# More accumulator banks for the feed-forward steps around a tile's end, and attention steps of the first two blocks laid out anew

## The chip, the cores and the metric

The kernel runs on one core of one Trainium2 chip. The metric is the device time of that core in microseconds (us), the median of three runs. Five engines work side by side: TensorE (PE; its weight loads are shown apart as PEld), VectorE (DVE), ScalarE (ACT), GpSimd (POOL) and SyncE (SP). Transfers run on DMA engines that all issuers share. TensorE writes its results to PSUM, eight banks of 128 x 512 float32; VectorE and ScalarE read them there.

## The reference

Attention over a window of the last 96 keys and the first 8 ("global") keys, with a linear distance bias, and then a gated feed-forward layer on the result:

```python
# q, k, v: (batch 4, heads 8, seq 768, dim 64)
scores = scale * q @ k.T  + bias            # bias = -slope[h] * distance
scores = where(keep, scores, -1e9)          # keep: local (0 <= i-j < 96) or global (j < 8)
a = exp(scores - max); a = a / (sum(a) + 1e-9)
attn = a @ v
x = attn as (3072 tokens, 512)
g = x @ w_gate                              # 512 x 1536
out = (g * sigmoid(g)) * (x @ w_val) @ w_out   # 1536 x 512
```

## The kernel before

The 3072 tokens are 8 tiles of 384 (two per batch element, here "block"). A tile takes 12 feed-forward steps, one for each 128 of the 1536 features. A step is four matmuls for the gate (`gps`), four for the value (`vps`), and then ScalarE and VectorE:

```python
def products(t, f, which, c0, c1, dst=None):
    ...
        if dst is None:
            dst = spare("gv"[which] + "ps")        # a bank, from the rotation "x"
    w = (wg, wv)[which]
    for c in range(c0, c1):
        nc.tensor.matmul(gv[f, which][:, 0:TB], lhsT=w[:, c, 128*f:128*f+128],
                         rhs=x_of(t)[:, c, :], start=(c == 0), stop=(c == NC - 1))

def gate_or_val(t, f, which, c0=0):
    products(t, f, which, c0, NC)
    dst = gv.pop((f, which))
    if which == 0:
        th = ...; nc.scalar.activation(out=th, in_=dst[:, 0:TB], func=AF.Tanh, scale=0.5)
        sl = ...; nc.vector.scalar_tensor_tensor(out=sl, in0=th, scalar=1.0,
                      in1=dst[:, 0:TB], op0=AluOp.add, op1=AluOp.mult)   # reads the gate's bank
    else:
        nc.vector.tensor_mul(hTs[t][:, f, :], dst[:, 0:TB], gv["sl"])    # reads the value's bank
```

`th` and `sl` have two buffers each. The banks: three (`x0` to `x2`) rotate for gates and values, four (`a0` to `a3`) for attention, and `o0` takes the output matmuls (`ops`):

```python
state = {"tags": ["a0", "a1", "a2", "a3"], "n": 0, "x": ["x0", "x1", "x2"]}

def spare(name, dt=FP32):
    tag = state["x"][gv.get("n", 0) % len(state["x"])]
    gv["n"] = gv.get("n", 0) + 1
    return single(name, tag, dt)          # waits until the tag's last readers are done
```

A list `later` holds VectorE, ScalarE and GpSimd work that is taken up piece by piece between steps. The attention of a block half ends with `values`: denominators (`den`) and numerators (`num`), copied to `ns` by ScalarE; VectorE turns the denominators (`dT`), inverts (`dR`), spreads them (`rb`) and scales, which gives the x of the next tile:

```python
later.append(lambda: self.invert(den))    # dT, dR
later.append(spread)                      # rb
if mul_eng is not nc.gpsimd:
    for side in range(2):
        later.append(lambda side=side: scale_num(side))   # xT
```

Block 0 is worked in two halves. Its second half is turned (transposed on TensorE, then copied from PSUM to `kT` and `qT`) pair by pair, two pairs sharing two banks; k and q of one pair lie in different banks:

```python
def trh(*units):
    def step():
        ks, qs = single("trs", "o0", FP16), spare("trs", FP16)
        for i, (hp, k_eng, q_eng) in enumerate(units):
            c = slice(TB * i, TB * i + TB)
            pairs[0, hp].transposes_half(1, [qs[:, c], ks[:, c]], k_eng, q_eng)  # turn, then copy
    return step

half1 = {(0, 1): [trh((0, A, A), (1, V, A))], (0, 2): [sch(0)],      # A: ScalarE, V: VectorE
         (0, 3): [sch(1), trh((2, V, A), (3, V, V))], (0, 5): [sch(2)], (0, 6): [sch(3)],
         (0, 7): [va(0, 0, 1)], (0, 8): [va(0, 1, 1)]}
```

A key `(t, f)` names the step of tile t after which the work is put: `sch` and `sc` make scores (with their exponentials and mask products), `va` the values, `tr` turns two pairs of a later block. Block 1 is worked in tile 1's steps; the last number of `ff` says how many groups of three output matmuls go behind each step:

```python
def first(t, b):
    return {(t, 3): [tr(b, 0), tr(b, 1)],
            (t, 5): [sc(b, (0, 0), (0, 1), (1, 0))],
            (t, 7): [tr(b, 2), tr(b, 3)],
            (t, 8): [sc(b, (1, 1), (2, 0), (2, 1))],
            (t, 9): [sc(b, (3, 0), (3, 1))],
            (t, 10): [va(b, 0, 0)], (t, 11, 1): [va(b, 1, 0)]}
...
(ff(1, 0, 6, (0, 0, 0, 1, 0, 1)) + ff(1, 6, 11, (1,)) + [(1, 11, 5)], first(1, 1)),
```

Weights come in four pieces of features (`load_w(0, 2)`, `(2, 4)`, `(4, 8)`, `(8, 12)`), each as two transfers for `wg` and two for `wv`: the first holds the rows of matmuls 0 and 1 of a burst, the second those of 2 and 3.

Of the kernel before, what the change touches and what calls it, by code (L numbers as in the profile page):

```python
# [37 lines left out]
def kernel(  # L38
# [223 lines left out]
    class Pair:  # L262
# [27 lines left out]
                in_=k3[:, 0, NG:2 * NG].unsqueeze(1).broadcast_to([128, NCH, NG]))  # L290


        def transposes_half(self, half, tr, k_eng, q_eng):
            hp = self.hp
            trq, trk = tr
            for st, dst in ((k16, trk), (q16, trq)):
                for j in range(J2):
                    for hi in range(2):
                        nc.tensor.transpose(  # L299
                            dst[64 * hi:64 * hi + 64, 128 * j:128 * j + 128],  # L300
                            st[:, half, 2 * hp + hi, D * j:D * j + D], ident)
            if half == 0:
                self.qT = sb2.tile([128, S], FP16, name="qT", tag="qT", bufs=NP)
                self.kT = kTs[hp]
            k3 = self.kT.rearrange("r (c m) -> r c m", m=128)
            t3 = trk.rearrange("r (j p) -> r p j", j=J2)
            pc = KC // J2
            cut = (TB - 3 * KC) // J2

            def part(c0, c1, m0, m1, p0):  # L310
                n = (m1 - m0) // J2
                k_eng(out=k3[:, c0:c1, NG + m0:NG + m1].rearrange("r c (p j) -> r c p j", j=J2),
                      in_=t3[:, p0:p0 + (c1 - c0) * n, :].rearrange(
                          "r (c p) j -> r c p j", c=c1 - c0))

            if half == 0:
                part(0, 3, 0, KC, 0)
                part(3, 4, 0, cut * J2, 3 * pc)
                nc.vector.tensor_copy(
                    out=k3[:, :, 0:NG],  # L320
                    in_=k3[:, 0, NG:2 * NG].unsqueeze(1).broadcast_to([128, NCH, NG]))
            else:
                part(3, 4, cut * J2, KC, 0)
                part(4, 6, 0, KC, pc - cut)
                part(6, 7, 0, S - 6 * KC, 3 * pc - cut)
            q_eng(
                out=self.qT[:, TB * half:TB * half + TB].rearrange("r (p j) -> r p j", j=J2),
                in_=trq.rearrange("r (j p) -> r p j", j=J2))
# [33 lines left out]
            else:  # L362
                exps()

        def scores(self, bk, mul_eng, put_off, sc):
            hp = self.hp
            for c in range(NCH):
                cb, col, q0, n = chunks[c]
                if cb != bk:
                    continue  # L370
                for hi in range(2):
                    r = slice(64 * hi, 64 * hi + 64)
                    keys = (kE[r, hp, :] if c == J and self.b > 1
                            else self.kT[r, 128 * c:128 * c + 128])
                    nc.tensor.matmul(  # L375
                        sc[hi][:, col:col + n], lhsT=keys,
                        rhs=self.qT[r, q0:q0 + n], start=True, stop=True)
            at = sb2.tile([128, 2, BANK], FP16, name="at", tag=f"at{bk}", bufs=NP)
            self.at[bk] = at

            def exps():
                for hi in range(2):
                    nc.scalar.activation(out=at[:, hi, :], in_=sc[hi][:, 0:BANK],  # L383
                                         func=AF.Exp, scale=scale)

            def mask():
                m = masks[:, 2 * hp:2 * hp + 2, :]
                if bk == 1:
                    for i in range(2):
                        a2 = at[:, :, WIN * i:WIN * i + WIN]  # L390
                        mul_eng.tensor_mul(a2, a2, m[:, :, WIN:2 * WIN])  # L391
                else:
                    o = WIN // 2 * bk
                    mul_eng.tensor_mul(at, at, m[:, :, o:o + BANK])  # L394

            if put_off:
                later.append(exps)
            else:
                exps()
            later.append(mask)  # L400

        def transposes_dma(self):
            b, hp = self.b, self.hp
# [8 lines left out]
    class Quad:  # L412
# [49 lines left out]
        def values(self, half, bank, mul_eng):  # L462
            den = bank("den")
            self.weigh(half, den, None)
            srcs = []
            for side in range(2):
                num = bank("num")
                self.weigh(half, num, side)
                src = sb2.tile([128, TB], FP32, name="ns", tag="ns", bufs=4)
                nc.scalar.copy(out=src, in_=num[:, 0:TB])  # L470
                srcs.append(src)

            def scale_num(side):
                mul_eng.tensor_mul(self.x_out(half, side), srcs[side], self.rb)  # L474

            def spread():
                self.spread()
                if mul_eng is nc.gpsimd:
                    for side in range(2):
                        scale_num(side)  # L480

            later.append(lambda: self.invert(den))
            later.append(spread)
            if mul_eng is not nc.gpsimd:
                for side in range(2):
                    later.append(lambda side=side: scale_num(side))

        def denominators(self, den):
            self.weigh(0, den, None)
# [8 lines left out]
    def both_values(b, half):  # L498
        two = [quads[b, g] for g in range(2)]
        for quad in two:  # L500
            den = spare("den")
            quad.weigh(half, den, None)
            quad.invert(den)
        srcs = {}
        for g, quad in enumerate(two):
            for side in range(2):
                num = bank("num")
                quad.weigh(half, num, side)
                src = sb2.tile([128, TB], FP32, name="ns", tag="ns", bufs=4)
                nc.scalar.copy(out=src, in_=num[:, 0:TB])  # L510
                srcs[g, side] = src

        def scale_num(eng, g, side):
            eng.tensor_mul(two[g].x_out(half, side), srcs[g, side], two[g].rb)  # L514

        def spread_first():
            two[0].spread()
            for side in range(2):
                scale_num(nc.gpsimd, 0, side)

        later.append(spread_first)
        later.append(two[1].spread)
        for side in range(2):
            later.append(lambda side=side: scale_num(nc.vector, 1, side))

    hTs = {}

# [86 lines left out]

    def p_tr(hp, kt, qt, q_eng):
        tr = [single("trs", t, FP16)[:, 0:TB] for t in (qt, kt)]
        pairs[0, hp].transposes_half(0, tr, V, q_eng)

    V, A = nc.vector.tensor_copy, nc.scalar.copy
    fill(16)  # L620
# [56 lines left out]
    def sc(b, *units):  # L677
        def step():
            for i, (hp, bk, *other) in enumerate(units):
                pair = pairs[b + 1 if other else b, hp]  # L680
                on_vector = pair.b < 2 or bk < 2 or hp % 2 == 0
                pair.scores(bk, nc.vector if on_vector else nc.gpsimd, bool(later),
                            [spare("sc") for _ in range(2)] if len(units) == 3 and i == 0
                            else banks("sc"))
        return step

    def va(b, g, half):
        return lambda: quads[b, g].values(half, bank, nc.vector if b < 2 else nc.gpsimd)

    def vas(b, half):  # L690
        return lambda: both_values(b, half)
# [1 line left out]
    def tr(b, hp):  # L693
        return pairs[b, hp].transposes

    def trh(*units):
        def step():
            ks, qs = single("trs", "o0", FP16), spare("trs", FP16)
            for i, (hp, k_eng, q_eng) in enumerate(units):
                c = slice(TB * i, TB * i + TB)  # L700
                pairs[0, hp].transposes_half(1, [qs[:, c], ks[:, c]], k_eng, q_eng)
        return step

    def sch(hp):
# [13 lines left out]
        return step  # L718

    def first(t, b):  # L720
        return {(t, 3): [tr(b, 0), tr(b, 1)],
                (t, 5): [sc(b, (0, 0), (0, 1), (1, 0))],
                (t, 7): [tr(b, 2), tr(b, 3)],
                (t, 8): [sc(b, (1, 1), (2, 0), (2, 1))],
                (t, 9): [sc(b, (3, 0), (3, 1))],
                (t, 10): [va(b, 0, 0)],
                (t, 11, 1): [va(b, 1, 0)]}
# [11 lines left out]
    def second(t, b):  # L739
        return {(t, 0): [sc(b, (0, 2), (1, 2))], (t, 3): [sc(b, (2, 2), (3, 2))],  # L740
                (t, 7): [vas(b, 1)]}

    half1 = {(0, 1): [trh((0, A, A), (1, V, A))], (0, 2): [sch(0)],
             (0, 3): [sch(1), trh((2, V, A), (3, V, V))], (0, 5): [sch(2)], (0, 6): [sch(3)],
             (0, 7): [va(0, 0, 1)], (0, 8): [va(0, 1, 1)]}

    def ff(t, f0, f1, n_out=(0,)):
# [1 line left out]

    stretches = [  # L750
        (ff(0, 0, 12), half1),
        (ff(1, 0, 6, (0, 0, 0, 1, 0, 1)) + ff(1, 6, 11, (1,)) + [(1, 11, 5)], first(1, 1)),
        (ff(2, 0, 12, (1,)) + ff(3, 0, 12, (1,)), both(2, 1)),
        (ff(4, 0, 12, (1,)) + ff(5, 0, 12, (1,)), both(4, 2)),
        (ff(6, 0, 12, (1,)), second(6, 3)),
# [25 lines left out]
            at_step(int(when) // NFF, int(when) % NFF, it)  # L781

    outs = [(t, i, part) for t in range(NT - 1) for i in range(3) for part in range(4)]
    def take(step_list):
        run_later(len(later))
        for step in step_list:
# [2 lines left out]
    for tiles, steps in stretches:  # L789
        for t, f, n_out in tiles:  # L790
            for ld in loads.pop((t, f), []):
                ld()
            if f == 0:
                run_later(len(later))
            for which in range(2):
                run_later(1)
                gate_or_val(t, f, which, NC if t == 0 and f < 2 else 0)
# [50 lines left out]
```

The softmax here doesn't subtract the row's maximum and nothing guards it: scores larger than these inputs give would overflow.

## Time and profile before

| | |
|---|---|
| time, median of three (least to most) | 245.12 us (245.11 to 245.51) |
| span of the profiled execution | 243.8 us |
| TensorE clock granted | 1.000 |
| idle of VectorE before `sl`, waiting for ScalarE's `th` | 40.1 us in all |
| idle of ScalarE before `th`, waiting for the gate burst | 52.0 us in all |
| DMA from memory | 28.67 MB |

An instruction's line in the timeline gives start, length, engine, source line, operation, what it writes and reads, the shapes, how many alike were merged, and in brackets the idle time of the engine before it with what ended that. A matmul's length is modelled and overlaps the next one's, so the pace of TensorE is read from starts. Line 299 turns block 0's halves, 539 makes gates and values, 552 and 556 are `sl` and `hT`, 375 scores, 213 weight transfers.

### The profile page before, as it was taken

Reading aid. Unit: us, or ns where it says so; the run is one execution under the profiler, and the core shown is the slowest. Engines: PE = TensorE matmul, PEld = TensorE weight load, DVE = VectorE, ACT = ScalarE, POOL = GpSimd, SP = SyncE. Lnnn points to the kernel's source line nnn. Section 1 sums busy time; section 2 is a strip of 40 time slices with the busy share of each in tenths; the row PEclk is TensorE's granted clock in tenths of the full one; section 3 lists DMA queues with packets and bytes.
Section 4 is the critical chain, followed back from the end, with each engine's and each line's share of the span. In section 5 each row is a group of like instructions: output and inputs, shape, how many; then the busy total and the mean of one; then the engine's idle time right before and its main releaser. Section 6 shows DMA issues by size and latency. Waiting matters only on the chain.

```text
span 243.8 us, 6052 instructions
## 1 busy us (share of the span) xinstructions
PE 235.8 (97%) x2428; PEld 136.0 (56%) x2428; DVE 167.1 (69%) x358; ACT 129.4 (53%) x291; POOL 96.8 (40%) x117
## 2 busy tenths in 40 slices
PE   7899898999999999999999999999999999999994
PEld 4555565566465556555565556555655565555543
DVE  5676749888886768776786658776785568555510
ACT  6637576868763655356446465367346534333221
POOL 8999674738980000996062252800032213000000
PEclk9999999999999999999999999999999999999999
DMA  7999999999996684699309778951101101110122
GB/s 142 167 190 198 180 206 198 205 154 126 153 121 117 122 144 100 42 157 148 60 3 140 143 142 94 66 70 44 46 0 46 43 0 46 44 41 5 43 88 86
DMA packets 84612, 25.10 MB, mean 103 GB/s; under 512 B 72816, under 2 KB 81640, under 8 KB 84584
## 3 DMA queue, kind: packets, MB, share of 16 engines
q0 software_dynamic: 65296, 14.05, 65.9%
q1 hardware_dynamic: 18728, 10.30, 16.7%
q8 instruction: 19, 0.31, 0.6%
q10 hardware_dynamic: 560, 0.36, 0.5%
q14 instruction: 9, 0.07, 0.1%
HBM read 28.67 MB, written 6.29 MB: 143 GB/s over the span
## 4 chain that ended last, share of the span: by engine, by line
PE 84%; DVE 7%; ACT 3%; DMA 2%; issue 1%; POOL 0%; DVEq 0%; POOLq 0%
PE gps L539 24%; PE ops L568 23%; PE vps L539 23%; PE sc L375 3%; PE num L439 3%; DMA q<-in_q_dram 2%; PE den L439 2%; DVE sl L552 2%; DVE hT L556 2%; PE sc L335 2%; DVE xT L474 1%; ACT at L357 1%; PE trs L273 1%; ACT th L550 1%; PE trs L299 1%
## 5 line engine op out<-in xcount | busy, mean ns | idle before, releaser
L552 DVE SCALAR_TENSOR_TENSOR sl<-th,gps 128x384 f32<-128x384 f32 x94 | 52.0, 553 | 40.1 <-ACT th L550 39.1
L539 PE MATMUL gps<-xT,wg 128*128 128x384 f16 x376 | 76.9, 327 | 0.4
L539 PE MATMUL vps<-xT,wv 128*128 128x384 f16 x376 | 76.5, 326 | 0.6 <-DVE sl L552 0.5
L550 ACT ACTIVATE th<-gps 128x384 f32<-128x384 f32 x94 | 46.7, 497 | 53.5 <-PE gps L539 52.0
L568 PE MATMUL ops<-wo,hT 128*128 128x512 f16 x276 | 72.8, 379 | 0.0
L556 DVE TENSOR_TENSOR hT<-vps,sl 128x384 f16<-128x384 f32 x94 | 52.0, 554 | 7.9
L539 PEld LDWEIGHTS <-wg 128*128 128x128 f16 x384 | 35.1, 98 | 31.2 <-issue 2.3
L539 PEld LDWEIGHTS <-wv 128*128 128x128 f16 x384 | 37.5, 98 | 26.8 <-issue 2.1
L568 PEld LDWEIGHTS <-hT 128*128 128x128 f16 x276 | 26.9, 98 | 23.9
L383 ACT ACTIVATE at<-sc 128x432 f16<-128x432 f32 x72 | 33.1, 539 | 12.2 <-PE sc L375 12.2
L514 POOL TENSOR_TENSOR xT<-ns,rb 128x384 f16<-128x384 f32 x10 | 9.8, 997 | 67.5 <-DVE rb L455 56.5
L171 POOL DMA_DIRECT2D vS<-in_v_dram x28 | 24.7, 896 | 5.3 <-DMA kst<-in_k_dram 3.8
L574 ACT ACTIVATE osb<-ops 128x512 f32<-128x512 f32 x23 | 13.7, 597 | 21.9 <-PE ops L568 21.9
L394 POOL TENSOR_TENSOR at<-at,masks 128x864 f16<-128x864 f16 x4 | 7.3, 1822 | 23.8 <-ACT at L383 19.1
L394 DVE TENSOR_TENSOR at<-at,masks 128x864 f16<-128x864 f16 x20 | 12.1, 604 | 5.4 <-ACT at L383 5.4
L194 POOL DMA_DIRECT2D kst<-in_k_dram x16 | 13.9, 885 | 2.3 <-PE vps L539 1.7
L357 ACT ACTIVATE at<-sc 128x432 f16<-128x432 f32 (+2 forms) x32 | 11.7, 445 | 5.6 <-PE sc L346 5.4
L194 POOL DMA_DIRECT2D qst<-in_q_dram x16 | 13.7, 877 | 0.2 <-issue 0.2
L510 ACT COPY ns<-num 128x384 f32<-128x384 f32 x20 | 8.1, 492 | 7.9 <-PE num L439 7.9
L439 PE MATMUL num<-at,vS 128*32 128x216 f16 (+6 forms) x560 | 11.1, 226 | 0.0
L391 DVE TENSOR_TENSOR at<-at,masks 128x432 f16<-128x432 f16 x24 | 8.1, 378 | 4.1 <-ACT at L383 4.1
L449 DVE STREAM_TRANSPOSE dT<-den 128x384 f32<-128x384 f32 x16 | 9.3, 581 | 1.4 <-PE den L439 0.9
(74 smaller groups left out, 180.2 us busy)
## 6 DMA issues: line engine op xcount, KB each, us to landing
out_dram<-osb SPq DMA_DIRECT2D x23, 256.0 KB
vS<-in_v_dram POOLq DMA_DIRECT2D x24, 120.0 KB, 5.4
wo<-in_moe_w_out_dram POOLq DMA_DIRECT2D x4, 384.0 KB, 10.4
qst<-in_q_dram POOLq DMA_DIRECT2D x16, 96.0 KB, 4.3
kst<-in_k_dram POOLq DMA_DIRECT2D x16, 90.0 KB, 4.9
wg<-in_moe_w_gate_dram POOLq DMA_DIRECT2D x4, 256.0 KB, 7.7
wv<-in_moe_w_val_dram POOLq DMA_DIRECT2D x4, 256.0 KB, 7.7
kst<-in_k_dram POOLq DMA_DIRECT2D x2, 384.0 KB, 12.0
```

Of the source, the lines that this page charges most:

```text
L171: nc.gpsimd.dma_start(out=vSs[b][NG:NG + n, c, :, :], in_=v[b, :, KC * c:KC * c + n, :].rearrange("h p d -> p h d"))
L194: nc.gpsimd.dma_start(out=st[b][p0:p0 + n, h // 2, :, h % 2, :], in_=src[b, h, 0:n * J].rearrange("(t p) d -> p t d", p=n))
L357: nc.scalar.activation(out=at[:, hi, 0:col + n], in_=sc[hi][:, 0:col + n], func=AF.Exp, scale=scale)
L383: nc.scalar.activation(out=at[:, hi, :], in_=sc[hi][:, 0:BANK], func=AF.Exp, scale=scale)
L394: mul_eng.tensor_mul(at, at, m[:, :, o:o + BANK])
L439: nc.tensor.matmul(dst[r, o:o + n], lhsT=ones[:, 0:32] if side is None else vals[:, 4 * g + j, side::2], rhs=pairs[b, 2 * g + j // 2].at[c ...
L539: nc.tensor.matmul(gv[f, which][:, 0:TB], lhsT=w[:, c, 128 * f:128 * f + 128], rhs=x_of(t)[:, c, :], start=(c == 0), stop=(c == NC - 1))
L550: nc.scalar.activation(out=th, in_=dst[:, 0:TB], func=AF.Tanh, scale=0.5)
L552: nc.vector.scalar_tensor_tensor(out=sl, in0=th, scalar=1.0, in1=dst[:, 0:TB], op0=AluOp.add, op1=AluOp.mult)
L556: nc.vector.tensor_mul(hTs[t][:, f, :], dst[:, 0:TB], gv["sl"])
L568: nc.tensor.matmul(ops, lhsT=hTs[t][:, f, 128 * i:128 * i + 128], rhs=wo[:, f, :], start=(f == 0), stop=(f == NFF - 1))
L574: nc.scalar.mul(out=osb, in_=ops, mul=0.5)
```

## The change

It has four parts, none of which changes what is computed.

1. Between step 9 of tile 0 and step 2 of tile 1 no output matmuls run and attention leaves its four banks alone. There gates and values rotate over seven banks (three and the four of attention) so that TensorE can run ahead of their readers.
2. At the start of that stretch, work for the next x that still waits in `later` is put ahead of the step's own `sl` and `hT`. At the start of a tile, only what its x needs is flushed.
3. In block 0's second half, all transposes of two pairs are issued ahead of their copies, and the banks are shared out so that one bank is read by few engines. For pairs 0 and 1 ScalarE makes every copy; for pairs 2 and 3 VectorE makes `kT` and ScalarE `qT`.
4. Block 1's turns and scores move one step earlier, so that the last two score steps stand two steps apart. The output groups move with them.

```diff
-        def transposes_half(self, half, tr, k_eng, q_eng):
+        def turn_half(self, half, tr):          # transposes only
...
+        def copy_half(self, half, tr, k_eng, q_eng):
...
-    def trh(*units):
+    def trh(h0, h1, by_engine):
         def step():
-            ks, qs = single("trs", "o0", FP16), spare("trs", FP16)
-            for i, (hp, k_eng, q_eng) in enumerate(units):
-                c = slice(TB * i, TB * i + TB)
-                pairs[0, hp].transposes_half(1, [qs[:, c], ks[:, c]], k_eng, q_eng)
+            b0, b1 = single("trs", "o0", FP16), spare("trs", FP16)
+            (a, b), (c, d) = [(t[:, 0:TB], t[:, TB:2 * TB]) for t in (b0, b1)]
+            k_eng = V if by_engine else A
+            pair_of = [(h0, (c, a)), (h1, (d, b))] if by_engine else [(h0, (b, a)), (h1, (d, c))]
+            for hp, tr in pair_of:
+                pairs[0, hp].turn_half(1, tr)
+            for hp, tr in pair_of:
+                pairs[0, hp].copy_half(1, tr, k_eng, A)
         return step
...
-        return {(t, 3): [tr(b, 0), tr(b, 1)],
-                (t, 5): [sc(b, (0, 0), (0, 1), (1, 0))],
-                (t, 7): [tr(b, 2), tr(b, 3)],
-                (t, 8): [sc(b, (1, 1), (2, 0), (2, 1))],
+        return {(t, 2): [tr(b, 0), tr(b, 1)],
+                (t, 4): [sc(b, (0, 0), (0, 1), (1, 0))],
+                (t, 6): [tr(b, 2), tr(b, 3)],
+                (t, 7): [sc(b, (1, 1), (2, 0), (2, 1))],
                 (t, 9): [sc(b, (3, 0), (3, 1))],
...
-    half1 = {(0, 1): [trh((0, A, A), (1, V, A))], (0, 2): [sch(0)],
-             (0, 3): [sch(1), trh((2, V, A), (3, V, V))], (0, 5): [sch(2)], (0, 6): [sch(3)],
+    half1 = {(0, 1): [trh(0, 1, False)], (0, 2): [sch(0)],
+             (0, 3): [sch(1), trh(2, 3, True)], (0, 5): [sch(2)], (0, 6): [sch(3)],
...
-        (ff(1, 0, 6, (0, 0, 0, 1, 0, 1)) + ff(1, 6, 11, (1,)) + [(1, 11, 5)], first(1, 1)),
+        (ff(1, 0, 5, (0, 0, 0, 0, 1)) + ff(1, 5, 11, (1,)) + [(1, 11, 5)], first(1, 1)),
...
+    def widen():
+        while later:
+            run_later(1)
+        x, n = state["x"], gv["n"]
+        state["x"] = ([x[(n + i) % 3] for i in range(3)]
+                      + [state["tags"][(state["n"] + i) % 4] for i in range(4)])
+        gv["n"] = 0
+
+    def narrow():
+        assert gv["n"] % 7 == 3
+        state["x"] = state["x"][0:3]
+        gv["n"] = 0
+
+    at_step(0, 9, widen)
+    at_step(1, 2, narrow)
...
             if f == 0:
-                run_later(len(later))
+                while any(fn.__name__ in ("spread", "spread_first", "scale") for fn in later):
+                    run_later(1)
```

Left out: the renaming that lets pieces of `later` be told apart, and who scales values of later blocks in a path that no later block takes.

More of the change, by code (lines that the diff above doesn't have):

```diff
@@ L301, in transposes_half @@
                             st[:, half, 2 * hp + hi, D * j:D * j + D], ident)
+        def copy_half(self, half, tr, k_eng, q_eng):
+            trq, trk = tr
+            hp = self.hp
             if half == 0:
@@ L363, in scores_half, with scores @@
                 exps()
-        def scores(self, bk, mul_eng, put_off, sc):
+        def scores(self, bk, mul_eng, sc):
             hp = self.hp
@@ L394, in mask @@
                     mul_eng.tensor_mul(at, at, m[:, :, o:o + BANK])
[L396 to L400, printed above, removed]
+            return exps, mask
         def transposes_dma(self):
@@ L473, in scale_num @@
             def scale_num(side):
-                mul_eng.tensor_mul(self.x_out(half, side), srcs[side], self.rb)
+                eng = mul_eng if side else nc.vector
+                eng.tensor_mul(self.x_out(half, side), srcs[side], self.rb)
             def spread():
@@ L478, in spread, with scale @@
                 if mul_eng is nc.gpsimd:
-                    for side in range(2):
-                        scale_num(side)
+                    scale_num(1)
             later.append(lambda: self.invert(den))
             later.append(spread)
-            if mul_eng is not nc.gpsimd:
-                for side in range(2):
-                    later.append(lambda side=side: scale_num(side))
+            for side in range(1 if mul_eng is nc.gpsimd else 2):
+                def scale(side=side):
+                    scale_num(side)
+                later.append(scale)
         def denominators(self, den):
@@ L521, in both_values, with spread, scale @@
         later.append(spread_first)
-        later.append(two[1].spread)
+        def spread():
+            two[1].spread()
+        later.append(spread)
         for side in range(2):
-            later.append(lambda side=side: scale_num(nc.vector, 1, side))
+            def scale(side=side):
+                scale_num(nc.vector, 1, side)
+            later.append(scale)
     hTs = {}
@@ L616, in p_tr @@
         tr = [single("trs", t, FP16)[:, 0:TB] for t in (qt, kt)]
-        pairs[0, hp].transposes_half(0, tr, V, q_eng)
+        pairs[0, hp].turn_half(0, tr)
+        pairs[0, hp].copy_half(0, tr, V, q_eng)
     V, A = nc.vector.tensor_copy, nc.scalar.copy
@@ L681, in step @@
                 on_vector = pair.b < 2 or bk < 2 or hp % 2 == 0
-                pair.scores(bk, nc.vector if on_vector else nc.gpsimd, bool(later),
-                            [spare("sc") for _ in range(2)] if len(units) == 3 and i == 0
-                            else banks("sc"))
+                exps, mask = pair.scores(
+                    bk, nc.vector if on_vector else nc.gpsimd,
+                    [spare("sc") for _ in range(2)] if len(units) == 3 and i == 0
+                    else banks("sc"))
+                if i == 0:
+                    exps()
+                else:
+                    later.append(exps)
+                later.append(mask)
         return step
     def va(b, g, half):
-        return lambda: quads[b, g].values(half, bank, nc.vector if b < 2 else nc.gpsimd)
+        return lambda: quads[b, g].values(half, bank, nc.vector)
     def vas(b, half):
```

## The prediction

> **What bounds the kernel now.** I read the page's totals first, then the tensor engine's timeline from 15 us on, then the vector and scalar timelines beside each gap found there. "Stream" below means the pace of back-to-back matmuls: four gate matmuls follow each other in 0.65 us, and so do three output matmuls of 512 columns.
>
> ```profile
> PE 235.8 (97%) x2428; PEld 136.0 (56%) x2428; DVE 167.1 (69%) x358; ACT 129.4 (53%) x291; POOL 96.8 (40%) x117
> ```
>
> TensorE is busy 97% of the span. From about 76 us on the chain of waits is one matmul burst after another at the stream's pace: gate, value and output bursts of 0.65 us follow with at most 0.1 us at a switch. Nothing the change does there could matter, and the change alters no order there. What can be won is the idle time of TensorE between 18 and 76 us. Three stretches carry it.
>
> The first is the turning of block 0's second half. There are two such steps, starting at 18.69 and 25.24 us. The second (first column: start, second: length, in us):
>
> ```profile
> 25.24 0.36 PE L299 MATMUL trs<-ident,k 128*64 128x128 f16 x6
> 25.43 0.34 PE L299 MATMUL trs<-ident,q 128*64 128x128 f16 x6
> 26.54 0.36 PE L299 MATMUL trs<-ident,k 128*64 128x128 f16 x6 [0.77 <-DVE kT L312]
> 26.70 0.36 PE L299 MATMUL trs<-ident,q 128*64 128x128 f16 x6
> 27.00 0.82 PE L539 MATMUL gps<-xT,wg 128*128 128x384 f16 x4
> 27.66 0.81 PE L539 MATMUL vps<-xT,wv 128*128 128x384 f16 x4
> ...
> 28.99 0.81 PE L539 MATMUL vps<-xT,wv 128*128 128x384 f16 x4
> ```
>
> The next pair's transposes wait for the copy out of the same bank. 24 transposes without a wait need 0.78 us (0.19 + 0.16 + 0.16 + 0.29); the step takes 1.76 us here, 1.73 us at 18.69.
>
> The second is where vector work of two attention groups meets the gates of tiles 0 and 1:
>
> ```profile
> 39.29 0.58 DVE L449 STREAM_TRANSPOSE dT<-den 128x384 f32<-128x384 f32 x1
> ...
> 39.91 0.23 DVE L450 RECIPROCAL dR<-dT 128x12 f32<-128x12 f32 x1
> 40.05 0.49 DVE L552 SCALAR_TENSOR_TENSOR sl<-th,gps 128x384 f32<-128x384 f32 x1
> ...
> 40.60 0.81 PE L539 MATMUL vps<-xT,wv 128*128 128x384 f16 x4 [0.46 <-DVE sl L552]
> ...
> 44.75 0.55 DVE L552 SCALAR_TENSOR_TENSOR sl<-th,gps 128x384 f32<-128x384 f32 x1 [0.30 <-ACT th L550]
> ...
> 45.41 0.56 DVE L556 TENSOR_TENSOR hT<-vps,sl 128x384 f16<-128x384 f32 x1
> ...
> 46.02 0.81 PE L539 MATMUL gps<-xT,wg 128*128 128x384 f16 x4
> ```
>
> From 36.1 to 44.5 us VectorE never rests. With three banks a value burst needs the previous step's `sl` and a gate burst the `hT` of two steps back. The starts 39.32, 40.60, 41.52, 42.45, 43.38 instead of one each 0.65 us give 0.62 + 0.27 + 0.28 + 0.29 = 1.46 us of idle TensorE.
>
> The third: two score steps stand one feed-forward step apart, and the second waits for banks that ScalarE's exponentials still read.
>
> ```profile
> 65.12 0.87 PE L375 MATMUL sc<-qT,kT 64*128 64x216 f16 x5
> 66.17 0.34 PE L375 MATMUL sc<-qT,kT 64*128 64x216 f16 x3 [0.17 <-ACT at L383]
> 66.44 0.82 PE L539 MATMUL gps<-xT,wg 128*128 128x384 f16 x4
> ```
>
> Eight matmuls take 1.31 us; twelve of them take 0.66 us at 62.41 us, so eight should take 0.47. That is 0.84 us too much. Last, tile 2's first gate burst takes 0.94 us at 74.98 (0.29 lost to its x).
>
> **What the Trainium skill says.** "PSUM — Partial Sum Buffer", section "PSUM bank collisions raise a hardware error", says that accesses are to be guarded by bank and quadrant, not by address. The trace agrees: the transposes at 26.54 us write other columns than the copy reads, and still wait. "TensorE: Matmul & The Clock Gate", section "Architectural detail", says that matmuls keep program order and that ACT and DVE are strict FIFO. The trace agrees: the burst at 40.60 us holds up everything behind it, and `sl` at 40.05 us sits behind the reciprocal. So a bank's release comes when VectorE's turn comes. "DMA: Bandwidth & Descriptors", section "Issuing engines are not separate DMA queues", says that all issuers share the same 16 engines; here the DMA row stands at 9 tenths over the first 70 us, so an earlier TensorE does not make weights arrive earlier.
>
> **The change, part by part.** No work is added or removed: the same matmuls, with TensorE's order differing in one place (block 1's transposes move one feed-forward step ahead of one gate, value and output burst), four copies moved from VectorE to ScalarE (three `kT`, one `qT`), and `rb`, `xT`, `xT` of the second group put ahead of `sl` and `hT`. Times below are those of before unless shifted.
>
> 1. *Transposes ahead of copies, first step.* 1.73 − 0.78 = 0.95 us gained at once. ScalarE now makes all copies of both pairs (about 1.8 us from 19.2, so to 21.05) ahead of `th`; `sl` then ends near 22.05, before the value burst that needs it (22.5). The gain holds: −0.95.
>
> 2. *Second step.* Also 0.98 us on paper, so the gate of step 4 would start at 25.1 instead of 27.0. But its weights are not there. The two last transfers of that quarter of the weights were issued at 18.77 and 19.48; the trace counts them complete at 26.4 (gate) and 27.7 (value). The issue below sits waiting for the latter:
>
> ```profile
> 28.02 0.70 POOL L213 DMA_DIRECT2D wv<-in_moe_w_val_dram x1 [0.64 <-DMA wv<-in_moe_w_val_dram]
> ```
>
> So gate 4 does its last two matmuls from 26.45, value 4 its last two from 27.75 to 28.08, and after gate 5 (0.65) value 5 starts at 28.73, against 28.99 before. All that is left of steps 1 and 2 together is −0.26.
>
> 3. *Seven banks and x first.* TensorE no longer stalls at 40.6 to 43.4; it runs on through steps 9, 10, 11 and tile 1's 0 and 1, ten bursts. At step 2 of tile 1 the rotation goes back to three banks, and its gate takes the bank of value 0 of tile 1, three bursts back. It then needs that `hT`, as before. Without stalls TensorE would be there at 46.02 − 1.46 = 44.56, or 44.53 without waits of 0.03. VectorE is not: its work in between is the same, only ordered otherwise. I lay it out by start-to-start times from the trace (independent 0.47; `sl` to `hT` 0.65, since `hT` needs `sl`; `dR` to `rb` 0.26; `rb` to `xT` 0.68). From `dT` 39.29: `dR` 39.91, `rb` 40.17, `xT` 40.85 and 41.31, `sl`9 41.78, `hT`9 42.43, then 1.12 per step: `hT`10 43.55, `hT`11 44.67, `hT` of tile 1's step 0 45.79, ending at 46.35. Before, it ended at 45.97. The old order hid the waits of `hT` on `sl` behind the other group's work; the new one shows them, and only the 0.30 us of idle at 44.75 is saved. The gate starts at 46.40, so +0.38. TensorE's 1.46 us of stalls become one stall of 1.87.
>
>    Block 1's transposes follow at once, at 47.80. VectorE enters them with its `hT` still to come (48.45 to 49.0), and has two `qT` copies of 0.95 before the `sl` that the second value burst behind them needs: `sl` ends at 51.44, and TensorE is there at 51.23. Another +0.26 with the semaphore. Less small waits of before, the part comes to +0.60.
>
> 4. *Score steps two apart.* The second score step comes 1.95 us later after the first; counted from its end, the exponentials take 0.17 + three pairs of 0.95 + one tanh of 0.49 = 3.5 us, and the second score step starts after two steps of 1.95, at 3.9. −0.84.
>
> 5. *Tile 2's x.* The order of VectorE there does not change, so the 0.29 stays. POOL's share of scaling moved to VectorE: block 0 and 1 had it on VectorE already, and no later group goes through this path. Nothing.
>
> Sum: −0.26 + 0.60 − 0.84 = −0.50 us, passed on unchanged by the saturated rest: 245.12 − 0.50 = 244.6 us.
>
> **Rivals.**
> - *All stalls vanish*: 0.95 + 0.98 + 1.46 + 0.84 = 4.2 us, 240.9 us. For it: seven banks hold three and a half steps, more than the 1.46 us to bridge. Against it: 27.7 for the weights, and the return to three banks while VectorE is behind.
> - *Weights arrive as needed, VectorE stays the bound*: −0.95 − 0.98 + 0.60 − 0.84, 243.0 us. For it: transfers might land sooner in another run. Against it: the DMA row is full.
> - *VectorE falls back further* after the transposes and gives up another microsecond: 245.6 us. For it: 5.1 of 6 us busy from 42 to 54 us. Against it: the stretch after 54 us has idle VectorE of 0.3 to 0.9 us in front of several instructions.
>
> **Range and chances.** The three terms are uncertain by some 0.5, 0.5 and 0.3 us, and the rivals reach from 243.0 to 245.6 without the first. Range 243.2 to 246.0. A gain over 2% needs 240.2, more than all stalls together; a loss over 2% needs a new stall of 5 us. Faster 0.04, same 0.93, slower 0.03.
>
> **What would show it.** Step 1 and 2: 24 transposes in about 0.8 us twice, then gaps inside gate 4 and value 4 that end near 26.4 and 27.7. Step 3: no gaps in the ten bursts from step 9, then one near 1.9 us before the gate of tile 1's step 2, released by `hT`. Step 4: eight score matmuls in about 0.5 us. I am wrong if the weights land a microsecond sooner, if the gate of step 2 waits for less than 1 us, or if the score steps keep a gap.

## The result and the profile after

| | before | changed |
|---|---|---|
| median of six runs of each, taken together | 245.12 us (244.91 to 245.60) | 244.54 us (244.11 to 245.62) |
| ratio to before | | 0.9978, 95% interval 0.9955 to 1.0000 |
| span of the profiled execution | 243.8 us | 243.8 us |

The first interval reaches 1.0000. A second set, of 22 runs, gave 0.9960 (0.9946 to 0.9974), which is clear of it; its medians are 245.58 and 244.79 us. So the change gains 0.2 to 0.4%, about 0.5 to 1.0 us by the ratios and 0.6 and 0.8 us by the medians. The profiled execution of the changed kernel was the slowest of its six, and its head (the part up to the first turn of block 0's second half) was late. These are ScalarE's lines at the start, first of before, then of the changed kernel (start, length, engine, line, operation, in brackets the idle time before it):

```profile
4.36 0.51 ACT L623 CAST q<-q 128x384 f16<-128x384 f32 x1 [0.42 <-DMA q<-in_q_dram]
```

```profile
5.76 0.51 ACT L632 CAST q<-q 128x384 f16<-128x384 f32 x1 [1.76 <-DMA q<-in_q_dram]
```

The first load of q landed 1.4 us later in the second, although both kernels issue it at 1.16 us. This belongs to the execution and not to the kernel: another execution of the changed kernel reached the first turn at 17.97 us. The first turn (18.69 us before, 20.13 after) is late by as much. So two profiles are not to be compared by their spans; they are compared stretch by stretch below.

The totals barely move, and one row of the changed kernel's groups says where TensorE now waits:

```profile
PE 235.6 (97%) x2428; PEld 136.0 (56%) x2428; DVE 165.5 (68%) x354; ACT 129.7 (53%) x295; POOL 96.7 (40%) x117
...
L547 PE MATMUL gps<-xT,wg 128*128 128x384 f16 x376 | 76.9, 327 | 1.9 <-DVE hT L564 1.7
```

Gate bursts waited 0.4 us in all before and 1.9 now; nearly all of it is a single wait for `hT`.

The second turn in the changed kernel, TensorE's timeline:

```profile
25.75 0.36 PE L299 MATMUL trs<-ident,k 128*64 128x128 f16 x6
25.94 0.33 PE L299 MATMUL trs<-ident,q 128*64 128x128 f16 x6
26.10 0.33 PE L299 MATMUL trs<-ident,k 128*64 128x128 f16 x6
26.27 0.33 PE L299 MATMUL trs<-ident,q 128*64 128x128 f16 x6
26.54 0.82 PE L547 MATMUL gps<-xT,wg 128*128 128x384 f16 x4
27.20 0.89 PE L547 MATMUL vps<-xT,wv 128*128 128x384 f16 x4
27.92 0.81 PE L547 MATMUL gps<-xT,wg 128*128 128x384 f16 x4
29.39 0.81 PE L547 MATMUL vps<-xT,wv 128*128 128x384 f16 x4 [0.65 <-DVE sl L560]
```

The 24 transposes take 0.79 us, about as foreseen (the four terms in the prediction add up to 0.80, not 0.78). Of the 1.9 us saved in both turns 0.82 is lost again at 29.39, where value 5 waits for `sl` of step 4. ScalarE made that `sl` late:

```profile
26.65 0.86 ACT L330 COPY qT<-trs 128x384 f16<-128x384 f16 x2 [0.31 <-PE trs L299]
27.39 0.97 ACT L361 ACTIVATE at<-sc 128x432 f16<-128x432 f32 x2
28.23 1.04 ACT L558 ACTIVATE th<-gps 128x384 f32<-128x384 f32 x2
```

Two copies and two exponentials stand ahead of the tanh, whose gate was done near 27.4.

The stretch with seven banks, TensorE and VectorE together:

```profile
40.30 0.23 DVE L450 RECIPROCAL dR<-dT 128x12 f32<-128x12 f32 x1
...
40.57 0.58 DVE L455 STREAM_TRANSPOSE rb<-dR 128x384 f32<-128x384 f32 x1
...
41.25 1.03 DVE L475 TENSOR_TENSOR xT<-ns,rb 128x384 f16<-128x384 f32 x2
...
42.20 0.55 DVE L560 SCALAR_TENSOR_TENSOR sl<-th,gps 128x384 f32<-128x384 f32 x1
...
44.27 0.81 PE L547 MATMUL vps<-xT,wv 128*128 128x384 f16 x4
...
46.22 0.56 DVE L564 TENSOR_TENSOR hT<-vps,sl 128x384 f16<-128x384 f32 x1
...
46.83 0.81 PE L547 MATMUL gps<-xT,wg 128*128 128x384 f16 x4 [1.74 <-DVE hT L564]
```

TensorE issues all ten bursts 0.65 us apart, up to 44.27. Then the gate of tile 1's step 2 starts 2.56 us later: a gap of 1.90 where four gaps of 1.46 in all had been.

And block 1, TensorE's timeline:

```profile
50.99 0.81 PE L547 MATMUL gps<-xT,wg 128*128 128x384 f16 x4
51.82 0.81 PE L547 MATMUL vps<-xT,wv 128*128 128x384 f16 x4
...
66.05 0.54 PE L379 MATMUL sc<-qT,kT 64*128 64x216 f16 x8
66.53 0.66 PE L547 MATMUL gps<-xT,wg 128*128 128x384 f16 x3
```

The last eight score matmuls take 0.48 us, where they had taken 1.31. The value burst at 51.82 is 0.18 late, which is new.

### The profile page after: what moved, and what is told of

Same layout as the page of the kernel before. It is cut to its first block, busy times and chain, and to the rows that moved or that the text cites. A ratio compares the mean times of both kernels' runs of the same rounds, so it can differ in the third digit from the quotient of the medians.

```text
span 243.8 us, 6052 instructions
## 1 busy us (share of the span) xinstructions
PE 235.6 (97%) x2428; PEld 136.0 (56%) x2428; DVE 165.5 (68%) x354; ACT 129.7 (53%) x295; POOL 96.7 (40%) x117
## 3 DMA queue, kind: packets, MB, share of 16 engines
q1 hardware_dynamic: 18728, 10.30, 17.1%
## 4 chain that ended last, share of the span: by engine, by line
PE 91%; DVE 4%; DMA 2%; ACT 1%; issue 1%; ACTq 0%; DVEq 0%
PE gps L547 26%; PE vps L547 25%; PE ops L576 23%; PE num L439 3%; PE sc L379 3%; PE sc L339 3%; PE den L439 2%; DMA q<-in_q_dram 2%; PE sc L350 2%; PE trs L299 1%; PE trs L273 1%; PE ops L592 1%; DVE xT L475 1%; DVE hT L564 1%; PE gvps L547 1%; DVE sl L560 1%
## 5 line engine op out<-in xcount | busy, mean ns | idle before, releaser
L547 PEld LDWEIGHTS <-wv 128*128 128x128 f16 x384 | 37.5, 98 | 26.9 <-issue 2.2
```

Of the source, the lines that this page charges most:

```text
L547: nc.tensor.matmul(gv[f, which][:, 0:TB], lhsT=w[:, c, 128 * f:128 * f + 128], rhs=x_of(t)[:, c, :], start=(c == 0), stop=(c == NC - 1))
```

## The experiments

Each kernel is read in three stretches that all start behind the head: A, from the first transpose of the first turn to value 5 of tile 0; B, from there to the gate of tile 1's step 6 (the same work in all kernels: two output groups, one turn, one score step); C, from there to tile 2's first gate. In us, from starts in TensorE's timeline:

| kernel | first turn at | A | B | C | ratio of times to before (95%) |
|---|---|---|---|---|---|
| before | 18.69 | 10.30 | 25.91 | 20.09 | 1 |
| changed | 20.13 | 9.25 | 26.44 | 19.24 | 0.9978 (0.9955 to 1.0000) |
| changed, again | 17.97 | 11.38 | 26.45 | 19.24 | 0.9960 (0.9946 to 0.9974) |
| turns only | 18.62 | 9.77 | 25.92 | 20.09 | 0.9989 (0.9972 to 1.0006) |
| spacing only | 18.34 | 11.35 | 26.04 | 19.24 | 0.9976 (0.9960 to 0.9991) |
| banks and x first only | 18.16 | 10.30 | 26.30 | 20.09 | 1.0011 (0.9987 to 1.0035) |
| changed without banks | 18.50 | 9.73 | 26.03 | 19.24 | 0.9956 (0.9937 to 0.9974) |
| banks, x not first | 18.32 | 9.87 | 25.64 | 19.24 | 0.9949 (0.9930 to 0.9967) |
| weights there | 18.60 | 9.26 | 26.42 | 19.24 | 0.9939 (0.9926 to 0.9953) |
| x made twice more | 18.64 | 9.95 | 27.62 | 19.24 | 1.0030 (1.0018 to 1.0042) |
| weights split, tanh first | 18.25 | 9.12 | 29.35 | 19.24 | 0.9933 (0.9917 to 0.9949) |
| banks, x not first, tanh first | 18.45 | 9.64 | 25.65 | 19.24 | 0.9920 (0.9887 to 0.9953) |
| same, one x on GpSimd | 18.55 | 10.06 | 25.65 | 19.24 | 1.0031 (1.0009 to 1.0052) |

B and C repeat to 0.03 us between kernels that are alike there, so they settle the small terms better than the times do. A varies from one execution to the next with the arrival of loads, so one A is not the mean of its kernel.

The theory at the start: turns, banks and spacing act one by one and add up; the banks alone lose, because VectorE sets the pace, and the turns gain little, because something else stands ready behind the wait removed. The rival: every wait taken away is a gain, and the small total has some other cause.

**Turns only.** The kernel before with this edit:

```diff
-half1 = {(0, 1): [trh((0, A, A), (1, V, A))], ... trh((2, V, A), (3, V, V))
+half1 = {(0, 1): [trh(0, 1, False)], ... trh(2, 3, True)     # trh: turn both pairs, then copy
```

> Before, with only the second-half turns changed (transposes of two pairs ahead of their copies). Theory: from the first transpose of the first turn to the start of value 5 of tile 0 takes 9.3 to 10.0 us instead of 10.30, held up in the second turn either by the weights (counted complete near 27.6) or by ScalarE, so the time falls by 0.3 to 1.0 us depending on how late the head of the execution is. Rival (each wait taken away is a gain): 8.3 us for the stretch and -1.9 us in the time. The stretch from value 5 to step 6 of tile 1 stays at 25.9 us and the rest at 20.1 us.

A fell by 0.53, not by 1.9, and B and C stayed. The time's interval holds 1, so the gain in time is not clear of noise; the ratio makes it 0.3 us. Here the head was early, and TensorE's timeline shows the weights at work:

```profile
25.02 0.50 PE L543 MATMUL gps<-xT,wg 128*128 128x384 f16 x2
26.03 0.50 PE L543 MATMUL gps<-xT,wg 128*128 128x384 f16 x2 [0.52 <-DMA wg<-in_moe_w_gate_dram]
26.37 0.49 PE L543 MATMUL vps<-xT,wv 128*128 128x384 f16 x2
27.40 0.50 PE L543 MATMUL vps<-xT,wv 128*128 128x384 f16 x2 [0.55 <-DMA wv<-in_moe_w_val_dram]
27.74 0.81 PE L543 MATMUL gps<-xT,wg 128*128 128x384 f16 x4
28.39 0.81 PE L543 MATMUL vps<-xT,wv 128*128 128x384 f16 x4
```

Gate 4 and value 4 both stop after two matmuls and go on at 26.03 and 27.40.

**Spacing only.** Block 1's entries of `first` one step earlier, and the output groups with them:

```diff
-(t, 3): [tr ..], (t, 5): [sc ..], (t, 7): [tr ..], (t, 8): [sc ..]
+(t, 2): [tr ..], (t, 4): [sc ..], (t, 6): [tr ..], (t, 7): [sc ..]
```

> Before, with only block 1's turns and scores one step earlier. Theory: the eight score matmuls of the last score step take 0.5 us instead of 1.31; from the gate behind the first score step to tile 2's first gate 19.25 us instead of 20.08; time -0.8 us, less up to 0.2 if VectorE is late for the second value burst behind the first turn of block 1. Rival (the wait moves to the next bank): the stretch stays near 20.0 and the time within 0.2 us of before.

C fell by 0.85. B rose by 0.13: the second value burst behind the first turn waits 0.18 for `sl`, without any change to the banks. Net 0.72 us; the time fell by 0.24%, some 0.6 us. (A is 11.35 because weights were late in that execution, with gaps of 0.46 and 0.59 us in gate 2 and value 4.)

**Banks and x first only.**

```diff
+    at_step(0, 9, widen)     # flush `later`, rotate over x0..x2 and a0..a3
+    at_step(1, 2, narrow)
```

> Before, with only the seven banks and the x work put first. Theory (VectorE sets the pace, the banks only move the stall): no gap in the ten bursts from step 9 of tile 0, then one of 1.8 to 1.9 us in front of the gate of step 2 of tile 1, released by hT; time +0.3 to +0.5 us. Rival (banks were the limit): the 1.46 us of gaps are won, time -1.0 us or more.

B rose by 0.39, with no gap in the ten bursts and one of 1.90 us after them. The median time rose by 0.29 us, an amount that its interval does not separate from zero; the stretch does.

**The changed kernel without the banks.** The two lines above taken out.

> The changed kernel without the switch to seven banks and back (nothing is put first at step 9 either); turns and spacing stay changed. Theory: the gaps of 0.62 + 0.27 + 0.28 + 0.29 us come back, the one of 1.9 us goes, from value 5 of tile 0 to the gate behind block 1's first scores takes 25.9 to 26.1 us instead of 26.44; time 0.4 to 0.6 us under the changed kernel's, about 1.1 us under before. Rival (seven banks help): 0.5 us or more above the changed kernel's time.

B is 0.41 shorter than in the changed kernel. The banks cost 0.4 us in either surrounding, so this part does add up. The times do not settle it: the median is 0.34 us under the changed kernel's first, but the ratio, 0.9956, is hardly under the 0.9960 of its second set.

**Banks, x not first.** The flush inside `widen` taken out, so `rb` and `xT` are again taken up between `sl` and `hT`:

```diff
     def widen():
-        while later:
-            run_later(1)
```

> The changed kernel with the seven banks, but the x work left where it was (taken up between sl and hT, as before). Theory (VectorE's exposed sl-to-hT waits cost the 0.4 us): from value 5 of tile 0 to the gate of step 2 of tile 1 takes 16.6 to 16.8 us, against 17.44 in the changed kernel and 17.03 in the one without the banks; a gap of about 0.5 us appears in the first gate of tile 1, where x comes late, and one of 0.6 to 0.8 us before the gate of step 2. Time about 0.6 us under the changed kernel's. Rival (the order does not matter, only VectorE's total): 17.4 us again, time as the changed kernel.

From value 5 to the gate of tile 1's step 2 it took 16.64 us, against 17.44 with x first and 17.03 without the banks. TensorE's timeline has both gaps:

```profile
41.13 0.65 PE L547 MATMUL gps<-xT,wg 128*128 128x384 f16 x3
42.12 0.32 PE L547 MATMUL gps<-xT,wg 128*128 128x384 f16 x1 [0.34 <-DVE xT L475]
...
43.58 0.81 PE L547 MATMUL vps<-xT,wv 128*128 128x384 f16 x4
44.83 0.81 PE L547 MATMUL gps<-xT,wg 128*128 128x384 f16 x4 [0.44 <-DVE hT L564]
```

The x comes late and TensorE loses 0.51 us on it (first line 41.13, fourth matmul 42.12). Yet the gate of step 2 comes sooner after value 5, since VectorE finishes the same work sooner: from `dT` to the `hT` that this gate needs it takes 5.72 us here and 6.53 with x first. So in this stretch the banks are worth 0.4 us, and putting x first costs 0.8. It puts instructions that need each other side by side: `rb` starts 0.27 us behind `dR`, `xT` 0.68 behind `rb` and `hT` 0.65 behind `sl`, where with other work between them VectorE starts something every 0.15 to 0.49 us. The time (median 244.01 us) is 0.5 us under the changed kernel's first median, but the intervals of the ratios overlap.

**Weights there.** Steps 4 and 5 of tile 0 read the weights of steps 2 and 3, which came earlier; features 512 to 767 of tile 0 are left out.

```diff
-lhsT=w[:, c, 128 * f:128 * f + 128]
+lhsT=w[:, c, 128 * fw:128 * fw + 128]     # fw = f - 2 for t == 0, f in (4, 5)
```

> The changed kernel with steps 4 and 5 of tile 0 reading the weights of steps 2 and 3, which came earlier (the features 512 to 767 of tile 0 are left out and others computed twice). Theory: no gap inside gate 4 and value 4 in any execution; then value 5 waits for sl of step 4, which ScalarE's copies and exponentials hold up, so from the first turn to value 5 takes 9.25 us whatever the head; time 0.3 to 0.5 us under the changed kernel's median. Rival (weights were the only limit): 8.3 us, time 1.2 us or more under.

With an early head A is 9.26, as in the changed kernel's late one, and value 5 waits 0.89 us for `sl` of step 4. So two limits stand close behind the turns: the weights, and 0.5 us behind those ScalarE's row of copies, exponentials and tanh. The time is 0.6 us under the changed kernel's first median, a little more than the 0.3 to 0.5 expected.

**x made twice more.**

```diff
-eng.tensor_mul(self.x_out(half, side), srcs[side], self.rb)
+for _ in range(3 if side and (self.b, self.g, half) == (0, 1, 1) else 1):
+    eng.tensor_mul(self.x_out(half, side), srcs[side], self.rb)
```

> The changed kernel with the last x product of block 0 made three times (two more vector instructions of about 0.54 us, 0.47 us start to start, same result). Theory (VectorE sets the pace up to the gate of step 2 of tile 1): from value 5 to that gate takes 17.44 + 0.94 = 18.4 us, and the time rises by 0.9 us. Rival (TensorE's or ScalarE's chain sets it): 17.4 to 17.6 us, time unchanged.

The gate came at 18.62 instead of 17.44: 1.18 us later, not 0.94. VectorE sets the pace here, and the size of one product was off: three writes of one x follow each other by about 0.60 us, not 0.47 (the four products take 2.21 us, 0.47 + 2 x 0.60 + 0.54). The time rose by more than the 0.9 foreseen: its median is 1.5 and 1.3 us above those of the changed kernel's two sets.

**Weights split, tanh first.** No banks; the third quarter of the weights in two halves; step 4's tanh ahead of the put-off exponentials.

```diff
-    load_w(4, 8)
+    load_w(4, 6)
+    load_w(6, 8)
...
+    if (t, f, which) != (0, 4, 0):
         run_later(1)
```

> The kernel without the banks (turns and spacing changed), with the weights of features 512 to 1023 loaded in two halves, so that those of steps 4 and 5 land sooner, and step 4's tanh ahead of the two exponentials put off. Theory: from the first turn to value 5 takes 8.4 to 8.8 us instead of 9.73, other stretches as they were; time about 1.0 us under the kernel without the banks, 2.2 us under before. Rival (a later wait takes the gain, such as the next weights): the stretch from value 5 on grows by as much, time within 0.3 us of the kernel without the banks.

Gate 4, value 4 and gate 5 ran without a gap, and value 5 came 0.70 us behind gate 5, so both limits went. A was 9.12, since step 2's weights came 0.70 late in that execution. The rival came true for the profiled execution; TensorE's timeline, step 8 of tile 0:

```profile
33.95 0.50 PE L547 MATMUL gps<-xT,wg 128*128 128x384 f16 x2
36.30 0.50 PE L547 MATMUL gps<-xT,wg 128*128 128x384 f16 x2 [1.84 <-DMA wg<-in_moe_w_gate_dram]
36.63 0.49 PE L547 MATMUL vps<-xT,wv 128*128 128x384 f16 x2
37.54 0.82 PE L547 MATMUL vps<-xT,wv 128*128 128x384 f16 x2 [0.42 <-DMA wv<-in_moe_w_val_dram]
```

The next weights were late by more than had been won (2.6 us in all): GpSimd issued the transfer that gate 8 waited for at 28.22 us, with four more issues ahead of it, where it did so at 26.10 in the kernel without the banks. Not all of B's 29.35 is weights. Right behind these waits the granted clock fell, in the page's row the 7:

```profile
PEclk9999997999999999999999999999999999999999
```

Between 37.5 and 40.2 us it was 0.50 on average, and from the third matmul of value 8 to the gate of step 10 TensorE took 4.07 us instead of 2.75. That is another 1.3 us, of which shorter waits for VectorE behind it gave back 0.6; why the clock fell is not shown. This was the slowest of 22 runs (246.49 us; the others lie from 242.89 to 244.89). The median is 243.84 us, 1.5 us under before in the same set. The kernel without the banks was 1.2 us under its own, so most of the 1.0 us that the theory put between the two is missing.

**The changed kernel again, and two attempts at a better one.** The second is seven banks with x not first, plus tanh first. The third puts one product of tile 2's x on GpSimd as well.

> The changed kernel once more, beside the next two. Theory: in an execution whose first load lands early (first turn near 18.5 us), gate 4 and value 4 of tile 0 wait for weights until about 26.0 and 27.3 us and the stretch from the first turn to value 5 takes 9.7 to 10.0 us; with a late first load (first turn near 20 us) it takes 9.25. From value 5 to the gate behind block 1's first scores 26.4 us either way. Time 0.4 to 0.9 us under before. Rival (the gain of the turns is whole when the head is early): 8.3 us.

> Seven banks, x work not put first, and step 4's tanh ahead of the two exponentials put off. Theory: with an early head nothing is gained over the kernel without the last part, since the weights rule (first turn to value 5 9.7 to 9.9 us); with a late head 0.5 us or more (8.4 to 8.9 us). Value 5 to the gate behind block 1's first scores 25.6 us. Time 0.0 to 0.4 us under the kernel with the banks and x not first, so about 1.5 us under before. Rival (ScalarE rules always): 0.6 us or more under.

> As the one before, with one of the four x products of block 1's first half (tile 2's x) on GpSimd instead of VectorE. Theory: tile 2's first gate burst loses no 0.29 us (0.66 us instead of 0.94), as VectorE reaches the last product 0.47 us earlier; time 0.3 us under the kernel before it. Rival (GpSimd's queue of loads, in which the product now stands and waits for rb, delays block 2's q and k): a wait of TensorE between 80 and 100 us, time the same or above.

The changed kernel's head was the earliest of all (first turn at 17.97), and it gained nothing by it: gate 2 waited 1.52 us for weights, then gate 4 and value 4 another 0.73 and 0.72, and value 5 started at 29.35, as it had with the late head (29.39). My 9.7 to 10.0 for A missed this; it left out the weights of step 2. This execution, too, was the slowest of its set (245.58 us, median 244.79), so neither profile of the changed kernel shows A as it is in a usual execution.

The second has the lowest ratio of all, 0.9920; A is bound by weights as expected. Its interval reaches down to 0.9887 and overlaps those of its neighbours, so only its gain over before, and not the last part's, is shown. It is the version I would keep.

The third lost, as its rival said. GpSimd's and TensorE's timelines:

```profile
60.15 1.71 POOL L194 DMA_DIRECT2D qst<-in_q_dram  x2
70.51 1.00 POOL L475 TENSOR_TENSOR xT<-ns,rb 128x384 f16<-128x384 f32 x1 [8.65 <-DVE rb L455]
71.46 1.79 POOL L194 DMA_DIRECT2D kst<-in_k_dram  x2
```

```profile
86.55 0.55 PE L379 MATMUL sc<-qT,kT 64*128 64x216 f16 x10
88.86 0.36 PE L379 MATMUL sc<-qT,kT 64*128 64x216 f16 x4 [1.76 <-DMA qT<-qst]
```

The product waits 8.65 us at the head of GpSimd's queue, the loads of block 2 wait behind it, and TensorE waits 1.76 us for `qT` at 88.86. Nor was the 0.29 us at tile 2's first gate won: that burst took 1.14 us, not 0.66.

## Why the prediction was right, and where it was not

- *The size and the class* held: −0.50 us foreseen; −0.58 and −0.79 by the medians of two sets, −0.54 and −0.98 by their ratios. The terms do not agree as closely as their sum: two of them were off by 0.2 to 0.3 us, and that the first set came within 0.1 us is partly luck.
- *Step 1, the first turn*: no gap was left in its transposes in any kernel that has it. From the first turn to the second it took 6.55 us before and 5.61 with turns only (24.23 − 18.62): 0.94 gained, 0.95 foreseen. At value 5 that gain does not show whole, since step 2's limit follows.
- *Step 2, the weights*: shown where the head was early. There the matmuls stop at the places foreseen, and go on at 26.03 and 27.40 (turns only), for 26.45 and 27.75. What I missed is the second limit: the profile of the changed kernel itself, with its late head, shows ScalarE holding value 5 and hardly any wait for weights. The term was −0.26; turns only gave −0.53 in its stretch, as the weights of value 4 landed 0.35 us sooner than in the execution that the prediction was read from.
- *Step 3, VectorE and the banks*: shown, and the layout of VectorE's work came out to within 0.03 us. From `dT` to `rb`, first `xT`, `sl` and the last `hT` I had 0.88, 1.56, 2.49 and 6.50 us; the trace has 0.88, 1.56, 2.51 and 6.53. The stall foreseen was 1.87, and it is 1.90. But I charged another 0.26 us behind the transposes to the banks. Spacing alone and the kernel without banks have it too, as 0.17 to 0.18: it belongs to the earlier turn of block 1. The banks with x first cost 0.40, not 0.60. The step took the order as given and priced the banks and x first as one; apart they are −0.4 and +0.8. Whether a later return to three banks would cost less was not tested.
- *Step 4, the score steps*: 0.85 gained in C, 0.84 foreseen; less 0.13 in B that belongs to it, 0.72.
- *Step 5*: the 0.29 at tile 2's first gate is still there, to 0.01.
- *The rival "all stalls vanish"* falls with the table, and *"VectorE falls back further"* with it. *"Weights arrive as needed"* was tried with the weights there: ScalarE's limit stood 0.5 us behind them.

With the terms as measured: −0.53 for the turns in an early execution, +0.40 for the banks, −0.72 for spacing, together −0.85, between the two ratios and a little beyond both medians. How much the turns are worth on average stays open, as it hangs on when loads land: in six of the seven profiled executions in which kernels with the changed turns waited for the weights of step 4, value 4 went on between 27.10 and 27.62 us and A was 9.64 to 10.06 (10.30 before); in the seventh it went on at 28.37, and A was 11.38. The times (turns only against before, and the kernel without the banks against spacing only) give 0.2 to 0.7 us, and neither is clear of noise.

## What to carry to other kernels

More banks let the producer run ahead, but where the rotation narrows again it meets the consumer where the consumer's own work has brought it; lay out the consumer's queue first, and put independent work between an instruction and the one that reads its result. Before counting a removed wait as a gain, look up when the next operands land and what stands ahead of the next reader in its queue. In a kernel of which TensorE is busy 97%, compare stretches between fixed points of its timeline: where no late load falls into them they repeat to a few hundredths of a microsecond, where times scatter by a whole one.

## What was not expected of the hardware

- The landing of the first q load differed by 1.4 us between two executions, and a head 2.2 us earlier (17.97 against 20.13, with q's cast at 4.72 and 5.76, so q's load is only a part of it) brought value 5 no sooner, since later loads set it.
- Vector instructions of 0.55 us followed each other by 0.47 us when independent (`hT` to the next `sl`), 0.65 when the second reads the first's result (`sl` to `hT`), and about 0.60 when they wrote the same place (worked out from one kernel).
- With one set of transfers split in two, it landed in time and the next set was issued later, the transfer that gate 8 needs by 2.1 us; the weights of step 8 then held gate 8 for 1.84 us in the profiled execution, and behind that wait TensorE's granted clock was 0.50 for 2.7 us.
